# One more landing place for weight words, and copies moved from VectorE to ScalarE in seven items of a fused attention and MLP kernel

## The chip, the cores and the metric

The kernel runs on one core of a Trainium2 chip. The core has TensorE (PE, matrix products into PSUM), VectorE (DVE), ScalarE (ACT), GpSimd (POOL) and SyncE (SP); POOL and SP also issue the DMA transfers here. The metric is the device time of one execution in microseconds, smaller is better; the time given is the median of several runs. One execution of the kernel was recorded by the profiler.

## The reference

Inputs are q, k and v in float32 (8 batches, 8 heads, 576 rows, 64 columns) and two weight matrices in float64. Linear attention is followed by a two-layer network with a self-made gate:

```python
q_s = softmax(q, axis=-1)                       # over the 64 columns
k_s = softmax(k, axis=2)                        # over the 576 rows
kv = einsum('bhsd,bhse->bhde', k_s, v)
x = einsum('bhsd,bhde->bhse', q_s, kv)          # then to 4608 tokens x 512
h = x @ w_in                                    # 512 x 2048
sp = maximum(h, 0) + log1p(exp(-abs(h)))        # softplus
out = (h * erf(sp)) @ w_out                     # 2048 x 512
```

## The kernel before

**Items.** The 4608 tokens are cut into 12 blocks of 384, and the 2048 inner columns into 4 groups of 512. A pair of block and group is an item, 48 in all, numbered n. Item n does its first products (`mm1`: x times a group of w_in into banks X, Y and Z of PSUM, evacuated into a tile H), then softplus and erf by ScalarE (`T`, `G`; tile G), then G times H by VectorE (`U`, L1077), and then its second products (`mm2`: G times a group of w_out into banks o). The loop at the end emits, for each n, the first products of item n, the gate of item n-1 and the second products of item n-2; steps of the attention for later blocks are put between (`pace`).

**Two arithmetics.** Items 0 to 4 (n < N32) run in float32. From item 5 on a value is split into a float16 upper half and a float16 remainder, and a product is three float16 products. There `mm1` uses seven smaller products in place of eight: twelve matmuls of 192 columns each, into Y, X, Z, X, X, Z, X. Bank X has one buffer and is written by five of the seven products. Copies and additions between them, by VectorE and ScalarE, build H: the copy of bank Y into H is L1009 on VectorE. G's upper half is a conversion to float16 (`ghi`, L1091, VectorE), its remainder a subtraction (`glo`, L1095, VectorE).

**Weights.** A weight arrives as a 64-bit float: two 32-bit words. Each of 8 weight groups (JOBS) comes in two loads of 1 MB; `wdecode` turns the words of one load into float32 by three integer operations of VectorE (L213, L216, L219), the steps `D0.0` to `D7.1` of the hand-written ORDER. The words land in places that are free at that time: the list `slots` holds them, `rw` and parts of weight tiles WT that are not in use yet, and `wload` gives the next place to the next load. The first eight loads are issued by SP, the others by POOL, each when a decoding has freed its place. After all decodings the weights' scales are found (`Z`) and the weights are split in halves (`S`, `R`; L299 by ScalarE and L300 by VectorE), most of it between items 4 and 9 (SPLITS).

**Order.** ORDER and the loop give the order in which the program is written. A scheduler then orders the instructions of each engine by priorities and by its own estimates; on the chip each engine runs its list in order and waits by semaphores only for what its instruction reads or overwrites. `tc.issue_after(...)` is a hint to the scheduler.

**Start.** SP loads k, q, v and the first words. VectorE makes maxima over k (L517, L518, L521), PE transposes them (kT), VectorE reduces (km) and PE spreads them over the rows (kB). Behind kB stand 46 matmuls without a use of their result, which warm the clock (L809).

Of the kernel before, what the change touches and what calls it, by code (L numbers as in the profile page):

```python
# [10 lines left out]
I32 = mybir.dt.int32  # L11
BF16 = mybir.dt.bfloat16
AF = mybir.ActivationFunctionType
ALU = mybir.AluOpType
# [28 lines left out]

N32 = 5
SPLITS = {4: "", 5: "S1 R1 S2", 6: "S3 R3 S4", 7: "S6 f2 f3", 8: "S5 R5", 9: "S7"}

SHARES = [2.51, 0, 0.16, 0.09, 1.58, 2.43, 1.12, 0.26, 0.29, 0.04, 0.78, 1.12, 0.16]
LEAD = 2.0
# [7 lines left out]
def attn_moe_kernel(  # L56
# [9 lines left out]
    nc = tc.nc  # L66
# [3 lines left out]
    P = 128  # L70
# [43 lines left out]
    WT = [  # L114
        cp.tile([P, 2 * (7 if which == "in" else 4) * 512], F16, name=f"wt{i}")
        for i, (which, g) in enumerate(JOBS)
    ]
# [33 lines left out]
    raws, stg = {}, {}  # L151
    wready = set()
    slots, nxt = [], [0]
# [5 lines left out]
    def wload():  # L159


        i = nxt[0]
        while i < NPC * NJ and slots:
            w = slots.pop(0)
            if i >= NPC * (NJ - 1 if w is None else NJ if w < 2 else w - 2):
                continue
            if w == -1:
                w, other = None, "x7"
            else:
                other = None  # L170
            which, g = wjobs[i // NPC]
            a = i % NPC
            if which == "in":
                src = w_in[a * 2 * P:(a + 1) * 2 * P, 2 * g * 512:2 * (g + 1) * 512]
            else:
                src = w_out[(4 * g + 2 * a) * P:(4 * g + 2 * a + 2) * P, :]
            if other:

                raws[i] = xp.tile([P, 2, 1024], I32, tag=other, name=f"raw_{i}")
            elif w is None:  # L180
                raws[i] = rw.bitcast(I32).rearrange("p (a n) -> p a n", a=2)
            else:
                raws[i] = WT[w][:, :4096].bitcast(I32).rearrange("p (a n) -> p a n", a=2)
            held[i] = -1 if other else w

            eng = nc.sync if i < LOADS.count("w") else nc.gpsimd
            eng.dma_start(raws[i], src.rearrange("(a p) n -> p a n", p=P))
            nxt[0] += 1
            return

    decoded = [None]

    def wdecode(i, part=None):


        jn, a = divmod(i, NPC)
        if jn not in stg:
            if jn + 2 < NJ:
                stg[jn] = WT[jn + 2][:, :4096].bitcast(F32)
            elif jn == NJ - 2:  # L200
                stg[jn] = xp.tile([P, 2048], F32, tag="x7", name=f"sg_{jn}")
            else:
                stg[jn] = rw
        d = stg[jn][:, a * 1024:(a + 1) * 1024].bitcast(I32)
        if part is None:
            r = raws[i].rearrange("p a n -> p (a n)").rearrange("p (n two) -> p n two", two=2)
        else:
            r = raws[i][:, :, 512 * part:512 * part + 512].rearrange(
                "p a (n two) -> p a n two", two=2
            )  # L210
            d = d.rearrange("p (a n) -> p a n", a=2)[:, :, 256 * part:256 * part + 256]
        lo, hi = r[..., 0], r[..., 1]
        nc.vector.tensor_scalar(  # L213
            d, hi, 5, 2, op0=ALU.logical_shift_left, op1=ALU.logical_shift_right,
        )
        nc.vector.scalar_tensor_tensor(  # L216
            d, lo, 29, d, op0=ALU.logical_shift_right, op1=ALU.bitwise_or
        )
        decoded[0] = nc.vector.scalar_tensor_tensor(  # L219
            d, hi, -(2**30), d, op0=ALU.bitwise_and, op1=ALU.bitwise_or  # L220
        )
        if part == 0:
            return
        raws.pop(i)
        h = held.pop(i)
        if h != -1:
            slots.append(h)
        wload()

    def whalf(jn, h):  # L230

        return WT[jn][:, h * 2048:(h + 1) * 2048]

    def wop(jn, h, i, n):

        o = h * WIN + i * 512
        return WT[jn][:, o:o + n * 512].rearrange("p (n c f) -> p n c f", n=n, c=2)
# [735 lines left out]
    def mm1(n, k):  # L973

        p, bk, g = seq[n]
        s = st[n]
        assert ("in", g) in wready
        x = x7[p * NBK + bk]  # L980
        jn = wjobs.index(("in", g))
        Th = T // 2
        if k == 0:
            s["H"] = ch.tile([P, FG, T], F32, tag="H", bufs=3, name=f"H_{n}")
        C = {(i, j): s["H"][:, 2 * i:2 * i + 2, Th * j:Th * j + Th]
             for i in range(2) for j in range(2)}

        def prod(b, wi, xi):
            new = b not in s
            if new:  # L990
                s[b] = psh.tile([P, 512], F32, tag=f"p{b}", name=f"p{b}_{n}")
            w = [wop(jn, h, wi, 1)[:, 0] for h in range(2)]
            for a in range(2):
                o = s[b][:, a * Th:(a + 1) * Th]
                for c in range(2):
                    for i, (wl, xl) in enumerate(((0, 0), (0, 1), (1, 0))):
                        nc.tensor.matmul(  # L997
                            o, w[wl][:, c, a * P:(a + 1) * P], x[:, xl, xi, c, :],
                            start=(new and a == 0 and c == 0 and i == 0),
                            stop=(c == 1 and i == 2), skip_group_check=True,  # L1000
                        )

        def bank2(b):
            return s[b][:, :T].rearrange("p (a t) -> p a t", a=2)

        add = nc.vector.tensor_tensor
        if k == 0:
            prod("Y", 1, 1)
            nc.vector.tensor_copy(C[0, 0], bank2("Y"))  # L1009
            prod("X", 0, 0)  # L1010
            add(C[0, 0], bank2("X"), C[0, 0], op=ALU.add)  # L1011
        elif k == 1:
            prod("Z", 6, 3)
            nc.scalar.copy(C[1, 1], bank2("Z"))
            prod("X", 3, 6)
            nc.scalar.copy(C[0, 1], bank2("X"))
        elif k == 2:
            prod("X", 5, 5)
            add(C[1, 1], bank2("X"), C[1, 1], op=ALU.add)  # L1019
        else:  # L1020
            prod("Z", 4, 2)
            add(C[0, 1], bank2("Z"), C[0, 1], op=ALU.add)  # L1022
            prod("X", 2, 4)
            nc.scalar.copy(C[1, 0], bank2("X"))  # L1024
# [27 lines left out]
    def flat(t):  # L1052
        return t.rearrange("p f t -> p (f t)")
# [34 lines left out]

    def ghi(n):
        s = st[n]  # L1090
        nc.vector.tensor_copy(flat(s["gh"]), flat(s["G"]))  # L1091

    def glo(n):
        s = st[n]
# [48 lines left out]

    steps = start()
    fn = dict(T=softplus, G=erf, U=gmul, I=ghi, O=glo)
    emitted_steps = set()
    done = set()
# [76 lines left out]
    for n in range(N32, N + 2):  # L1224
# [3 lines left out]
        for i in range(4):  # L1228
# [7 lines left out]
            if m2 and i < 3:  # L1236
                tok(f"M{n - 2}.{i}")
                pace(n + (i + 1) / NTT)
        for o in SPLITS.get(n, "").split():
            tok(o)  # L1240
# [35 lines left out]
```

## Time and profile before

| | |
|---|---|
| time, median of 3 runs | 832.39 us (832.22 to 834.11) |
| the profiled execution | 833.08 us, span 831.2 us |
| TensorE busy | 804.8 us (97%) |
| VectorE busy | 626.6 us (75%) |
| ScalarE busy | 503.4 us (61%) |
| moved by DMA | 61.56 MB, 74 GB/s in the mean |

Rows of the timeline give start and length in us, the engine, the line of the program, the operation, output and input, and a count; a bracket holds the engine's idle time before the row and what ended it. Rows of groups give the busy us of all, the mean ns of one, and the idle time before them. Rows of windows give for each engine its busy us in the stretch, then the clock that TensorE was granted (1.00 is full), the mean busy share of the DMA engines and the GB/s that they moved. Rows of DMA issues give the queue, the count, the KB of one and the median us from issue to landing.

### The profile page before, as it was taken

What the parts mean: (1) busy time and instruction counts of PE and PEld (TensorE: products, weight loads), DVE (VectorE), ACT (ScalarE), POOL (GpSimd) and SP (SyncE); (2) the same over time, 40 slices, a digit from 0 to 9 for tenths busy, and PEclk for the clock granted to TensorE, in tenths of its full rate; (3) what the DMA queues carried; (4) which work ended last, traced back from release to release, by engine and by line L of the source; (5) the groups of instructions that cost most, each with busy time, mean ns of one, the idle gap of its engine ahead of it and who ended that gap; (6) DMA issues with size and microseconds to landing.
All of it is one profiled execution on the core that took longest, in us unless ns stands there. A gap on an engine that the chain in (4) does not pass through costs nothing.

```text
span 831.2 us, 15665 instructions
## 1 busy us (share of the span) xinstructions
PE 804.8 (97%) x6610; PEld 546.8 (66%) x6610; DVE 626.6 (75%) x894; ACT 503.4 (61%) x644; POOL 15.9 (2%) x37
## 2 busy tenths in 40 slices
PE   5999999999999999999999999999999999999996
PEld 4555556666676667667767667767776777767762
DVE  6999899999997869757976779867875656544643
ACT  3697678886576656546744746645764555544442
POOL 2101000000000000000000000000000000000000
PEclk9999999999999999999999999999999999999999
DMA  9995721041146206111451205311220100100101
GB/s 248 409 227 181 194 51 39 2 108 40 51 71 140 77 6 137 56 26 27 100 123 39 64 1 109 89 27 27 65 51 15 39 1 2 39 1 2 39 1 39
DMA packets 141349, 61.56 MB, mean 74 GB/s; under 512 B 130528, under 2 KB 132576, under 8 KB 141280
## 3 DMA queue, kind: packets, MB, share of 16 engines
q1 hardware_dynamic: 139104, 52.18, 25.0%
q0 software_dynamic: 2176, 8.39, 2.8%
q8 instruction: 52, 0.85, 0.4%
q14 instruction: 17, 0.14, 0.1%
HBM read 45.09 MB, written 9.44 MB: 66 GB/s over the span
## 4 chain that ended last, share of the span: by engine, by line
PE 55%; DVE 27%; ACT 9%; issue 3%; DMA 3%; SPq 3%; POOL 0%; ACTq 0%; DVEq 0%; POOLq 0%
PE o L1123 27%; PE pX L997 13%; PE pZ L997 7%; DVE G L1077 3%; PE pY L997 3%; ACT G L348 3%; ACT L348 3%; DVE H L1095 3%; DVE wt L300 2%; SPq L419 2%; DVE x L300 2%; DMA q<-in_q_dram 2%; DVE H L1091 2%; DVE x L392 1%; PE x L679 1%
## 5 line engine op out<-in xcount | busy, mean ns | idle before, releaser
L1123 PE MATMUL o<-wt,H 128*128 128x512 f16 x1548 | 356.0, 379 | 1.7 <-DVE H L1091 1.3
L997 PEld LDWEIGHTS <-wt 128*128 128x128 f16 x3612 | 300.0, 98 | 36.5 <-issue 14.3
L1123 PEld LDWEIGHTS <-H 128*128 128x128 f16 x1548 | 149.2, 98 | 154.0 <-DVE H L1091 1.8
L997 PE MATMUL pX<-x,wt 128*128 128x192 f16 x2064 | 198.8, 246 | 3.8 <-DVE H L1019 2.4
L348 ACT ACT_TABLE_LOAD x104 | 133.4, 1283 | 7.0 <-DVE H L1022 5.2
L1077 DVE SCALAR_TENSOR_TENSOR G<-G,small,H 128x1536 f32<-128x1536 f32 x44 | 79.9, 1817 | 53.3 <-ACT G L348 53.0
L1024 ACT COPY H<-pX 128x384 f32<-128x384 f32 x43 | 20.4, 475 | 144.5 <-PE pX L997 141.4
L997 PE MATMUL pZ<-x,wt 128*128 128x192 f16 x1032 | 100.6, 246 | 0.0
L348 ACT ACTIVATE G<-H,U 128x768 f32<-128x768 f32 (+1 forms) x58 | 71.0, 1241 | 22.1 <-DVE H L1022 21.5
L1095 DVE TENSOR_TENSOR H<-G,H 128x1536 f16<-128x1536 f32 x43 | 75.5, 1755 | 0.8
L348 ACT ACTIVATE G<-G 128x1536 f32<-128x1536 f32 x48 | 71.3, 1485 | 0.5
L997 PE MATMUL pY<-x,wt 128*128 128x192 f16 x516 | 49.6, 246 | 0.3 <-DVE H L1009 0.3
L453 ACT ACTIVATE x<-x 128x384 f32<-128x384 f32 (+1 forms) x52 | 16.2, 397 | 48.4 <-PE x L679 48.4
L1022 DVE TENSOR_TENSOR H<-pZ,H 128x384 f32<-128x384 f32 x43 | 23.7, 551 | 26.2 <-PE pZ L997 26.2
L1009 DVE COPY H<-pY 128x384 f32<-128x384 f32 x43 | 23.8, 553 | 25.7 <-PE pY L997 25.7
L299 ACT ACTIVATE x<-x 128x768 f16<-128x768 f32 (+1 forms) x44 | 32.9, 765 | 15.2 <-DVE x L392 15.1
L1091 DVE CAST H<-G 128x1536 f16<-128x1536 f32 x43 | 41.1, 957 | 0.8
L300 DVE SCALAR_TENSOR_TENSOR x<-x,x 128x768 f16<-128x768 f32 (+1 forms) x44 | 37.3, 852 | 3.2 <-ACT x L299 3.2
L1139 DVE TENSOR_SCALAR ob<-o,V 128x512 f32<-128x512 f32 x29 | 21.7, 748 | 20.4 <-PE o L1123 20.4
L1011 DVE TENSOR_TENSOR H<-pX,H 128x384 f32<-128x384 f32 x43 | 23.9, 555 | 13.2 <-PE pX L997 12.4
L464 DVE TENSOR_REDUCE q_m<-q 128x16 f32<-128x1024 f32 x14 | 17.0, 1217 | 17.0 <-DMA q<-in_q_dram 16.8
L1036 PE MATMUL pX<-x,wt 128*128 128x384 f32 x80 | 28.3, 488 | 0.2 <-DVE wt L219 0.2
(183 smaller groups left out, 790.4 us busy)
## 6 DMA issues: line engine op xcount, KB each, us to landing
out_dram<-ob SPq DMA_DIRECT2D x32, 256.0 KB, 2.3
vbuf<-in_v_dram SPq DMA_DIRECT2D x56, 128.0 KB, 3.2
q<-in_q_dram SPq DMA_DIRECT2D x56, 128.0 KB, 3.2
k<-in_k_dram SPq DMA_DIRECT2D x56, 128.0 KB, 3.2
wt<-in_moe_w_out_dram POOLq DMA_DIRECT2D x5, 1024.0 KB, 6.6
wt<-in_moe_w_in_dram SPq DMA_DIRECT2D x4, 1024.0 KB, 11.9
wt<-in_moe_w_out_dram SPq DMA_DIRECT2D x2, 1024.0 KB, 15.5
H_raw<-in_k_dram SPq DMA_DIRECT2D x2, 512.0 KB, 4.8
```

Source lines behind the costliest of these rows:

```text
L299: nc.scalar.activation(hi, src, AF.Copy, scale=s)
L300: nc.vector.scalar_tensor_tensor(lo, src, s, hi, op0=ALU.mult, op1=ALU.subtract)
L348: i = nc.scalar.activation(out_, in_, func, **kw)
L997: nc.tensor.matmul(o, w[wl][:, c, a * P:(a + 1) * P], x[:, xl, xi, c, :], start=(new and a == 0 and c == 0 and i == 0), stop=(c == 1 and i ...
L1009: nc.vector.tensor_copy(C[0, 0], bank2("Y"))
L1011: add(C[0, 0], bank2("X"), C[0, 0], op=ALU.add)
L1022: add(C[0, 1], bank2("Z"), C[0, 1], op=ALU.add)
L1036: nc.tensor.matmul(ph[:, :T], w[:, c, a * P:(a + 1) * P], x[:, c, :], start=(c == 0), stop=(c == NC4 - 1),)
L1077: nc.vector.scalar_tensor_tensor(flat(s["G"]), flat(s["G"]), GA32 if n < N32 else GA[:, g:g + 1], flat(s["H"]), op0=ALU.mult, op1=ALU.mult,)
L1091: nc.vector.tensor_copy(flat(s["gh"]), flat(s["G"]))
L1095: nc.vector.tensor_tensor(flat(s["gl"]), flat(s["G"]), flat(s["gh"]), op=ALU.subtract)
L1123: nc.tensor.matmul(o, s[gt][:, a, ts_], w[wl][:, a, :], start=(first_ and a == 0 and i == 0), stop=(last_ and a == FG - 1 and i == 2),)
```

## The change

First, behind the decoding of load 6 (the seventh, `D3.0`) one more place is put into `slots`: the upper thousand words of two weight tiles, WT[1] and WT[3] (columns 4096 to 6144), which together hold the 1 MB of one load. Load 11 goes there in two transfers; it is decoded in two halves of 512 words a row (six operations in place of three). The loads after it each take the place that the load before them had. Second, in items 5 to 11 (RELIEF) the copy of bank Y and the conversion to G's upper half are done by ScalarE in place of VectorE.

```diff
+RELIEF = range(5, 12)
...
             if w == -1:
                 w, other = None, "x7"
-            else:
-                other = None
+            elif w == -2:
+                w, other = None, "upper"
...
+            if other == "upper":
+                raws[i] = [WT[o][:, 4096:6144].bitcast(I32) for o in (1, 3)]
+            elif other:
...
             eng = nc.sync if i < LOADS.count("w") else nc.gpsimd
-            eng.dma_start(raws[i], src.rearrange("(a p) n -> p a n", p=P))
+            src = src.rearrange("(a p) n -> p a n", p=P)
+            if other == "upper":
+                for h in range(2):
+                    eng.dma_start(raws[i][h], src[:, h])
+            else:
+                eng.dma_start(raws[i], src)
...
+        if type(raws[i]) is list:
+            pieces = [(r, d[:, 512 * h:512 * h + 512]) for h, r in enumerate(raws[i])]
...
+        for r, d in pieces:
...
         wload()
+        if i == 6:
+            slots.append(-2)
+            with tc.issue_after(decoded[0].ins):
+                wload()
...
-            nc.vector.tensor_copy(C[0, 0], bank2("Y"))
+            (nc.scalar.copy if n in RELIEF else nc.vector.tensor_copy)(C[0, 0], bank2("Y"))
...
-        nc.vector.tensor_copy(flat(s["gh"]), flat(s["G"]))
+        (nc.scalar.copy if n in RELIEF else nc.vector.tensor_copy)(flat(s["gh"]), flat(s["G"]))
```

The scheduler makes more of it than the diff shows. The first place is POOL's list at the start of the program; wt_90 and wt_92 are WT[1] and WT[3], and the last two rows are the first loads that POOL issues after the start. Before:

```order
L444 MEMSET vtail 64x8
L411 MEMSET wt_89 128x16
L406 MEMSET v_1_114 128x16
L857 TENSOR_TENSOR q_0_134<-H_raw_q,q_0_m 128x4x128 x2
L857 TENSOR_TENSOR q_1_135<-G_raw_1_108,q_1_m 128x4x128 x2
L443 MEMSET vtail 64x520
L444 MEMSET vtail 64x8
L187 DMA rw<-in_moe_w_out_dram 128x2x1024
```

After:

```order
L467 MEMSET vtail 64x8
L434 MEMSET wt_89 128x16
L197 DMA wt_90<-in_moe_w_in_dram 128x1024
L429 MEMSET v_1_114 128x16
L197 DMA wt_92<-in_moe_w_in_dram 128x1024
L880 TENSOR_TENSOR q_0_134<-H_raw_q,q_0_m 128x4x128 x2
L880 TENSOR_TENSOR q_1_135<-G_raw_1_108,q_1_m 128x4x128 x2
L466 MEMSET vtail 64x520
```

The two transfers of load 11 stand ahead of everything that POOL computes, and no wait stands in front of them.

The second place is ScalarE's list from the softplus of item 7 on. H_1217 and G_1459 (after: H_1221, G_1463) are item 7's tiles, H_1466 (H_1470) and G_1650 (G_1654) are item 8's, H_1658 is item 9's. Before:

```order
L348 ACTIVATE G_1459<-G_1459 128x1536
L1014 COPY H_1466<-pZ_1523 128x2x192
L299 ACTIVATE wt_94<-wt_96,small 128x1024
L1016 COPY H_1466<-pX_1481 128x2x192
L299 ACTIVATE wt_94<-wt_96,small 128x1024
L654 CAST asc<-qT_0_1568 128x512
L654 CAST asc<-qT_1_1600 128x512
L1024 COPY H_1466<-pX_1481 128x2x192
L348 ACT_TABLE_LOAD
L348 ACTIVATE G_1650<-H_1466,U_673 128x1536
L299 ACTIVATE wt_96<-rw,small 128x2048
```

After:

```order
L371 ACTIVATE G_1463<-G_1463 128x1536
L1037 COPY H_1470<-pZ_1527 128x2x192
L1039 COPY H_1470<-pX_1485 128x2x192
L322 ACTIVATE wt_96<-rw,small 128x2048
L1114 CAST H_1221<-G_1463 128x1536
L677 CAST asc<-qT_1_1604 128x512
L677 CAST asc<-qT_0_1572 128x512
L1047 COPY H_1470<-pX_1485 128x2x192
L1032 COPY H_1658<-pY_1659 128x2x192
L371 ACT_TABLE_LOAD
L371 ACTIVATE G_1654<-H_1470,U_678 128x1536
```

The long split of 2048 columns moved from behind item 8's softplus to a place ahead of the conversion of item 7's G; that conversion, new here, stands between the two copies of item 8's bank X, and the copy of item 9's bank Y ahead of item 8's softplus.

More of the change, by code (lines that the diff above doesn't have):

```diff
@@ L166, in wload @@
                 continue
+            other = None
             if w == -1:
                 w, other = None, "x7"
-            else:
-                other = None
+            elif w == -2:
+                w, other = None, "upper"
             which, g = wjobs[i // NPC]
@@ L176, in wload @@
                 src = w_out[(4 * g + 2 * a) * P:(4 * g + 2 * a + 2) * P, :]
-            if other:
+            if other == "upper":
+                raws[i] = [WT[o][:, 4096:6144].bitcast(I32) for o in (1, 3)]
+            elif other:
                 raws[i] = xp.tile([P, 2, 1024], I32, tag=other, name=f"raw_{i}")
@@ L204, in wdecode @@
         d = stg[jn][:, a * 1024:(a + 1) * 1024].bitcast(I32)
-        if part is None:
-            r = raws[i].rearrange("p a n -> p (a n)").rearrange("p (n two) -> p n two", two=2)
-        else:
-            r = raws[i][:, :, 512 * part:512 * part + 512].rearrange(
-                "p a (n two) -> p a n two", two=2
-            )
[L211 to L221, printed above, removed]
+        if type(raws[i]) is list:
+            pieces = [(r, d[:, 512 * h:512 * h + 512]) for h, r in enumerate(raws[i])]
+        elif part is None:
+            pieces = [(raws[i].rearrange("p a n -> p (a n)"), d)]
+        else:
+            pieces = [(
+                raws[i][:, :, 512 * part:512 * part + 512],
+                d.rearrange("p (a n) -> p a n", a=2)[:, :, 256 * part:256 * part + 256],
+            )]
+        for r, d in pieces:
+            if part is None:
+                r = r.rearrange("p (n two) -> p n two", two=2)
+            else:
+                r = r.rearrange("p a (n two) -> p a n two", two=2)
+            lo, hi = r[..., 0], r[..., 1]
+            nc.vector.tensor_scalar(
+                d, hi, 5, 2, op0=ALU.logical_shift_left, op1=ALU.logical_shift_right,
+            )
+            nc.vector.scalar_tensor_tensor(
+                d, lo, 29, d, op0=ALU.logical_shift_right, op1=ALU.bitwise_or
+            )
+            decoded[0] = nc.vector.scalar_tensor_tensor(
+                d, hi, -(2**30), d, op0=ALU.bitwise_and, op1=ALU.bitwise_or
+            )
         if part == 0:
```

## The prediction

> **What bounds the kernel now.** I read the engine shares first, then the busy times over the items that the change touches, then TensorE's timeline for its gaps, and last the first 26 us, because the built order puts a part of the change there.
>
> ```profile
> PE 804.8 (97%) x6610; PEld 546.8 (66%) x6610; DVE 626.6 (75%) x894; ACT 503.4 (61%) x644; POOL 15.9 (2%) x37
> ```
>
> TensorE (PE) is busy for 97% of the span: a change is worth only what it takes from PE's idle time or adds to it. Next the busy times from the first product of item 5 to that of item 12, cut in the timeline where an item's first product (pY) starts; items 5 and 6 are woven together, so the first window holds both.
>
> ```profile
> core 0: us, PE busy (x) PEld busy (x) DVE busy (x) ACT busy (x) POOL busy (x), PEclk, DMA share, GB/s
> 132.40:158.75 26.35, 25.52 (x198) 18.48 (x197) 26.29 (x32) 21.18 (x23) 0.00 (x0) 1.00 0.03 13
> 158.75:178.24 19.49, 18.66 (x206) 13.51 (x205) 19.42 (x31) 15.96 (x18) 0.63 (x2) 1.00 0.27 61
> 178.24:193.93 15.69, 15.69 (x133) 11.53 (x131) 15.69 (x30) 10.29 (x12) 0.00 (x0) 1.00 0.33 75
> 193.93:212.89 18.96, 17.55 (x155) 11.69 (x154) 17.96 (x23) 12.81 (x20) 0.00 (x0) 1.00 0.34 91
> 212.89:229.81 16.92, 15.78 (x130) 11.33 (x129) 16.58 (x22) 10.53 (x13) 0.00 (x0) 1.00 0.01 5
> 229.81:247.36 17.55, 17.55 (x203) 12.77 (x201) 15.93 (x27) 13.52 (x15) 0.63 (x2) 1.00 0.31 70
> ```
>
> VectorE (DVE) has next to no slack until 230 us, ScalarE (ACT) is busy for three quarters, and PE's clock is granted in full. What PE loses to that stands in its timeline; a bracket holds the idle time before the row and what ended it.
>
> ```profile
> 136.00 1.15 PE L997 MATMUL pY<-x,wt 128*128 128x192 f16 x12 [0.27 <-DVE H L1009]
> 137.67 1.16 PE L997 MATMUL pX<-x,wt 128*128 128x192 f16 x12 [0.51 <-DVE H L1011]
> ...
> 169.12 0.75 PE L564 MATMUL kv<-vbuf,k 128*64 128x65 f32 x16 [0.64 <-ACT k L348]
> ...
> 203.14 0.66 PE L661 MATMUL qT<-ident,q 128*128 128x128 f32 x4 [1.41 <-ACT x L453]
> ...
> 227.51 0.65 PE L543 MATMUL kB<-ident,km 128*128 128x128 f32 x4 [1.14 <-DVE km L532]
> ```
>
> These sum to 0.27 + 0.51 + 0.64 + 1.41 + 1.14 = 3.97 us. Modelled ends hide a little more (12 products are drawn 1.15 us long, though the next group follows after 0.99 where nothing waits): 5 x 0.16 more, so **4.8 us** is all that a perfect relief of DVE can win in these items.
>
> **The change, part by part.** *The load.* In the source it stands behind the seventh decoding. In the built order its two halves stand on POOL's queue between two small memsets at the program's start, and wait for nothing. The memset in question is the first row below; the others are the loads that POOL issues before the change, and one of SP's.
>
> ```profile
> 2.00 0.12 POOL L406 MEMSET v<- 128x16 f32 x1
> ...
> 30.03 0.89 POOL L187 DMA_DIRECT2D rw<-in_moe_w_out_dram  x1 [6.96 <-DVE x_e L127]
> ...
> 64.95 0.71 POOL L187 DMA_DIRECT2D rw<-in_moe_w_in_dram  x1 [29.50 <-DVE wt L219]
> ```
>
> ```profile
> 20.28 2.29 SPq L187 DMA_DIRECT2D raw<-in_moe_w_in_dram  x1
> ```
>
> ```profile
> rw<-in_moe_w_out_dram POOLq DMA_DIRECT2D x1, 1024.0 KB, 9.9
> ...
> raw<-in_moe_w_in_dram SPq DMA_DIRECT2D x1, 1024.0 KB, 23.7
> ...
> rw<-in_moe_w_in_dram POOLq DMA_DIRECT2D x1, 1024.0 KB, 5.4
> ```
>
> So what came at 64.95 now comes at about 2 us, and there k and q are on their way:
>
> ```profile
> 4.88 0.69 DVE L517 TENSOR_TENSOR asc<-H_raw 128x512 f32<-128x512 f32 x1 [4.88 <-DMA H_raw<-in_k_dram]
> ...
> 6.78 0.69 DVE L517 TENSOR_TENSOR asc<-H_raw 128x512 f32<-128x512 f32 x1 [0.76 <-DMA H_raw<-in_k_dram]
> ...
> 8.28 0.68 DVE L521 TENSOR_TENSOR asc<-asc,kt 64x512 f32<-64x512 f32 x1 [0.35 <-DMA kt<-in_k_dram]
> ```
>
> ```profile
> 4.00:6.00 2.00, 0.00 (x0) 0.00 (x0) 1.09 (x2) 0.00 (x0) 0.00 (x0) 1.00 1.13 348
> 6.00:8.00 2.00, 0.00 (x0) 0.00 (x0) 1.14 (x3) 0.00 (x0) 0.00 (x0) 1.00 1.19 200
> ...
> 30.00:35.00 5.00, 5.00 (x17) 2.96 (x16) 5.00 (x11) 4.78 (x15) 1.87 (x3) 1.00 1.03 409
> ```
>
> DVE's first maxima wait three times for k, and the DMA engines are full meanwhile (shares over 1). A load of POOL's doesn't queue behind SP's: the one issued at 30.03 landed 9.9 us later, near 40, the one that SP had issued at 20.28 after 23.7, at 44. So the new 1 MB takes its part from k. Its price is at most its own time: 1.05 MB at the 409 GB/s of 30 to 35 us is 2.6 us, at the mean of 348 and 200 it is 3.8; at least it is nothing, if k's rows pass first. Alone, such a load took 5.4 us, 2.8 more than its transfer; I put 1.8 of that ahead of the data, which then flow from 3.8 us. At half the rate from there k's second half lands some 1.5 us later, its tail (the wait at 8.28) about 2.1, and q, behind it, up to 2.6. I take **2.2 us**, near the full transfer, since the landings show sharing.
>
> Does PE lose all of it? The maxima are followed by a chain without a hole: 46 matmuls that warm the clock stand behind kB, made from the maxima, and the first item waits for a DVE that is full from 16 us on.
>
> ```profile
> 11.89 6.71 PE L809 MATMUL warm<-ident 128*128 128x256 f16 x46
> ...
> 25.86 1.53 PE L1036 MATMUL pX<-x,wt 128*128 128x384 f32 x4 [0.24 <-DVE wt L219]
> ```
>
> So 25.86 becomes 28.1. SP's later words shift with it and stay off the path.
>
> One rule speaks against this change: the Trainium skill (DMA: Bandwidth & Descriptors, Queues, rings and completion order) has every DMA engine alternate between queues by whole packets, about 9 to 17 descriptors long. By it and the page's 436 GB/s (Anatomy of one DMA) POOL's 1 MB would pass ahead of most of k, an estimate of 2.4 us for the loss and 0.2 on top of the sum below. The two landings, 9.9 and 23.7 us, agree with alternation; no row shows its grain.
>
> *What the early words bring.* One wait of DVE's, in the second-last pair of decodings, goes, since each later load moves up one place:
>
> ```profile
> 97.10 0.69 DVE L213 TENSOR_SCALAR rw<-wt 128x1024 int32<-128x1024 int32 x1 [3.83 <-DMA wt<-in_moe_w_out_dram]
> ```
>
> ```profile
> 100.00:120.00 20.00, 19.49 (x80) 10.11 (x79) 18.74 (x42) 15.28 (x34) 0.00 (x0) 1.00 0.23 53
> ```
>
> The last load still waits for the decoding before it, so part of the 3.83 us comes back there. PE has its products of items 3 and 4 queued and idles 0.51 us in the whole window behind it, and the weights' scales wait for matmuls that stand in PE's order at 111 us. I price this at 0, with 0.5 us as the most. The decoding in halves costs DVE three more instructions:
>
> ```profile
> 24.30 0.69 DVE L216 SCALAR_TENSOR_TENSOR wt<-rw,wt 128x512 int32<-128x512 int32 x1
> ...
> 78.99 1.22 DVE L216 SCALAR_TENSOR_TENSOR wt<-rw,wt 128x1024 int32<-128x1024 int32 x1
> ```
>
> Twice 0.69 against 1.22 is 0.16 us for an operation, some 0.5 us for three. PE's second products of items 1 and 2 cover it; without that cover it is 0.5 us more.
>
> *Copies and upper halves in items 5 to 11.*
>
> ```profile
> L1091 DVE CAST H<-G 128x1536 f16<-128x1536 f32 x43 | 41.1, 957 | 0.8
> L1009 DVE COPY H<-pY 128x384 f32<-128x384 f32 x43 | 23.8, 553 | 25.7 <-PE pY L997 25.7
> ```
>
> ```profile
> L348 ACT ACTIVATE G<-G 128x1536 f32<-128x1536 f32 x48 | 71.3, 1485 | 0.5
> L1016 ACT COPY H<-pX 128x384 f32<-128x384 f32 x43 | 20.6, 480 | 3.5 <-DVE G L1077 1.5 <-PE pX L997 1.4
> L629 ACT CAST rw<-q 128x1024 f16<-128x1024 f32 x10 | 10.4, 1047 | 2.1 <-DVE q L478 2.1
> ```
>
> DVE loses 7 x (0.957 + 0.553) = 10.6 us. ACT's price for the cast isn't in the trace: 1.485 us (erf on as many elements) to 1.57 (1.047 x 1.5); I take 1.5. So ACT gains 7 x (1.5 + 0.48) = 13.9 us. Over the 115 us of the six windows DVE goes from 111.9 busy us to 101.3 (88%), ACT from 84.3 to 98.2 (85%). Neither is the bound by its sum, but ACT now waits in order: the cast needs G's product from DVE, and behind the cast stand copies of bank X, which PE needs before its next product there.
>
> To price that I laid the built order of PE, ACT and DVE on the durations of before's rows, each instruction after its engine's previous one and after what it reads. Without the shift at the start, the first product comes at 158.7 for item 7 (before 158.75), 177.4 for item 8 (178.24), 194.1 for item 9 (193.93), 212.3 for item 10 (212.89), 227.9 for item 11 (229.81), 245.6 for item 12 (247.36). Gained are the wait at 227.51, since DVE reaches km with a copy and a cast less in front, and half of the one at 203.14, since a long split of ACT's moves ahead. Lost is about 0.7 us in item 8, where PE waits for an addition of DVE's that now stands behind a split of 2048 elements and G's lower half; the waits at 136 and 137.67 become one of 1.2 us and one of 0.4. The sum is **-1.8 us**; the bounds are -4.8 (all idle gone) and, above, the second rival.
>
> *Sum.* 2.2 + 0 - 1.8 = +0.4 us. The profiled execution took 833.08 us (span 831.2), so its like takes 833.5; the median of the three runs is 832.39, and I forecast **832.8**, which is no change: 0.3% of this time, about what a measurement of this kernel can tell from none, is 2.5 us.
>
> **The rivals.** *First, faster:* the load slips in front of nothing, because k's small rows are served first, and the relief wins most of its 4.8 us. For it: PE's five idles all name DVE or ACT behind DVE. Against it: the 9.9 us landing. With 0 and -3.6 the time is 828.8; it needs more than 2.5 us in all. *Second, slower:* ACT becomes the bound in items 5 to 11. Place: the copies of bank X behind the casts. For it: the kernel's own waits at 169.12 and 203.14 are for ACT already. Against it: second products, 2.6 us a piece, stand between most X products. If PE waits half a cast in each of seven items, that is 7 x 0.75 = 5.2 us in place of the gain, and with the start 832.4 + 2.2 + 5.2 = 839.8. It decides from 0.3 us an item, 2.1 us in all, that the walk has missed. *Third, slower:* the load costs its whole transfer, 2.6 to 3.8 us, and the relief turns into other waits of the same size: 835.0 to 836.2. *That the change doesn't do what it says* is part of the forecast: the load isn't behind the seventh decoding.
>
> **How the numbers follow.** Forecast, both terms nearly cancelling (830 to 834.8): 0.63. First rival 0.14, second 0.12, third 0.11. The range takes the first rival's middle and the third whole, and leaves the second out: 829.0 to 836.2. Faster by over 0.3% is the first rival and a sliver of the forecast, 0.15; slower the second and third, 0.23; within 0.3% the rest, 0.62.
>
> **What would show it.** Right at the start: DVE's tail row of k at about 10.4 in place of 8.28, the warming matmuls at 14, the first item's product at 28.1; if they stand where they stood, the first term is wrong. No wait for words near 97 us, and a short one before the last decoding. From item 5's first product to item 12's 113.2 us in place of 115.0, ACT near 85% there; an idle of PE's in each item that names ACT would show the second rival. From item 12 on nothing should change but the offset.

## The result, and the profile after

| | before | after |
|---|---|---|
| time, median | 833.25 us (832.22 to 834.90) | 840.06 us (838.64 to 841.30) |
| ratio of the times | | 1.0078, 95% interval 1.0059 to 1.0097 |
| the profiled execution | 833.08 us, span 831.2 us | 841.30 us, span 839.5 us |
| VectorE, ScalarE busy | 626.6, 503.4 us | 618.4, 515.2 us |

The change makes the kernel 0.8% slower, and 840.06 us lies outside the predicted range of 829.0 to 836.2. Where the 8.2 us between the two profiled executions arise is read from TensorE's timelines: the start of each item's first product (pY) after, less the same start before, worked out from the two. The profiled execution is the slowest of the change's four, so its parts add up to more than the 6.8 us between the medians.

| at the start of | first product on x | item 5 | 12 and 13 | 14 | 15 | 16 | 30 to 47 |
|---|---|---|---|---|---|---|---|
| later by (us) | 4.86 | 4.75 | 4.69 | 5.58 | 6.98 | 8.23 | 8.2 |

So the program's start costs 4.9 us, items 5 to 12, for which the relief was made, give nothing, and items 13 to 15 cost another 3.5 us. These three places are shown in turn.

**The start.** The timelines of VectorE, GpSimd and TensorE after, in this order:

```profile
6.37 0.69 DVE L540 TENSOR_TENSOR asc<-H_raw 128x512 f32<-128x512 f32 x1 [0.40 <-DMA H_raw<-in_k_dram]
...
13.02 0.68 DVE L544 TENSOR_TENSOR asc<-asc,kt 64x512 f32<-64x512 f32 x1 [5.51 <-DMA kt<-in_k_dram]
```

```profile
2.00 0.68 POOL L197 DMA_DIRECT2D wt<-in_moe_w_in_dram  x1
...
2.73 0.55 POOL L197 DMA_DIRECT2D wt<-in_moe_w_in_dram  x1
```

```profile
16.63 7.60 PE L832 MATMUL warm<-ident 128*128 128x256 f16 x46
...
30.72 1.56 PE L1059 MATMUL pX<-x,wt 128*128 128x384 f32 x4
```

The words' two transfers are issued at 2 us. The two halves of k are as early as before (6.37 us against 6.78), but VectorE waits 5.51 us for k's tail and reads it at 13.02 us in place of 8.28. The DMA issues of the first 16 us, after and then before (KB of one transfer, median us from issue to landing), and the DMA queues from 6.5 to 8.0 us after (packets, MB, share of the engines; q0 is POOL's queue, q1 is SP's):

```profile
H_raw<-in_k_dram SPq DMA_DIRECT2D x2, 512.0 KB, 4.5
wt<-in_moe_w_in_dram POOLq DMA_DIRECT2D x2, 512.0 KB, 8.9
...
kt<-in_k_dram SPq DMA_DIRECT2D x2, 128.0 KB, 11.1
```

```profile
kt<-in_k_dram SPq DMA_DIRECT2D x2, 128.0 KB, 6.4
```

```profile
q0 software_dynamic: 102, 0.38, 84.0%
q1 hardware_dynamic: 263, 0.07, 20.3%
```

The tail lands 11.1 us after its issue in place of 6.4. In the window in which it is due, POOL's queue moves 0.38 MB in 102 packets and SP's 0.07 MB in 263: packets of the tail hold one row of 256 bytes, those of the words nearly 4 KB in the mean. SP's queue keeps the larger number of packets and gets a sixth of the bytes.

**Items 5 to 12.** The windows of the six stretches from item 5's first product to item 12's are summed in the first row; then TensorE's largest idles there.

```profile
sum 114.90, PE 111.24 PEld 79.68 DVE 104.27 ACT 94.41 POOL 1.26; mean PE 18.54 PEld 13.28 DVE 17.38 ACT 15.74 POOL 0.21
```

```profile
141.54 1.15 PE L1020 MATMUL pX<-x,wt 128*128 128x192 f16 x12 [0.76 <-DVE H L1034]
...
144.34 1.15 PE L1020 MATMUL pX<-x,wt 128*128 128x192 f16 x12 [0.16 <-ACT H L1039]
...
173.60 0.76 PE L587 MATMUL kv<-vbuf,k 128*64 128x65 f32 x16 [0.70 <-ACT k L371]
...
181.65 0.62 PE L587 MATMUL kv<-vbuf,k 128*64 128x65 f32 x13 [0.31 <-DMA vbuf<-in_v_dram]
...
199.84 1.15 PE L1020 MATMUL pX<-x,wt 128*128 128x192 f16 x12 [0.74 <-DVE H L1042]
...
208.17 0.65 PE L684 MATMUL qT<-ident,q 128*128 128x128 f32 x4 [0.94 <-ACT x L476]
```

The stretch takes 114.90 us against 114.96 before (247.36 less 132.40). VectorE is busy for 91% of it and ScalarE for 82%. The waits of 1.14 us (km) and 0.27 us are gone and that of 1.41 us is 0.94, but 0.74 us at an addition of VectorE's and 0.31 us for v are new. PE's idle time falls from 4.21 to 3.66 us (114.90 - 111.24, and the same from the windows before), and its busy time, in which the ends are modelled, rises by 0.49. What this rise hides isn't shown; the stretch is as long as it was.

**Items 13 to 15.** The chain from item 11's conversion to the q tail, on ScalarE, VectorE and SP's queue in order of time, after and then before:

```profile
260.53 1.47 ACT L1114 CAST H<-G 128x1536 f16<-128x1536 f32 x1 [1.14 <-DVE G L1100]
...
261.91 0.70 ACT L652 CAST asc<-qt 128x256 f16<-128x256 f32 x2
...
262.03 1.76 DVE L1118 TENSOR_TENSOR H<-G,H 128x1536 f16<-128x1536 f32 x1 [0.83 <-ACT H L1114]
263.71 0.75 DVE L653 TENSOR_TENSOR asc<-qt,asc 128x256 f16<-128x256 f32 x2
...
264.49 1.23 SPq L655 DMA_TRANSPOSE qt<-asc  x1
...
267.65 0.42 DVE L541 TENSOR_TENSOR asc<-asc 128x256 f32<-128x256 f32 x1 [2.72 <-DMA qt<-asc]
```

```profile
255.94 2.95 SPq L632 DMA_TRANSPOSE q<-rw  x1
...
256.01 0.71 ACT L629 CAST asc<-qt 128x256 f16<-128x256 f32 x2 [1.30 <-DVE kvh L607]
...
256.76 0.75 DVE L630 TENSOR_TENSOR asc<-qt,asc 128x256 f16<-128x256 f32 x2
...
258.99 1.26 SPq L632 DMA_TRANSPOSE qt<-asc  x1
...
262.08 0.43 DVE L518 TENSOR_TENSOR asc<-asc 128x256 f32<-128x256 f32 x1 [2.13 <-DMA qt<-asc]
```

The conversion (L1114) waits 1.14 us for G's product, and the subtraction that makes G's remainder on VectorE (L1118) waits 0.83 us for the conversion. Behind the remainder stands the subtraction for the q tail (L653), which before (L630) came ahead of it. It ends at 264.46, and 0.03 us later the transposing transfer of the tail starts, 0.8 us late beyond the offset of 4.69. Before, this transfer started when SP's transpose ahead of it had ended, at 258.90. The two casts of the q tail stand behind the conversion on ScalarE and are 5.90 us later than before, but they end at 262.61, so the transfer doesn't wait for them. VectorE's row behind the transposes is 0.9 us late beyond the offset, and with it the additions to bank X that stand behind it in VectorE's order. Then TensorE after, its one row of before that answers to the 2.19 us, VectorE's wait for the next q after and before, and the windows after around the start of item 15 (the column behind POOL's is the granted clock):

```profile
278.41 1.15 PE L1020 MATMUL pX<-x,wt 128*128 128x192 f16 x12 [0.76 <-ACT H L1039]
...
300.92 1.60 PE L1020 MATMUL pX<-x,wt 128*128 128x192 f16 x12 [2.19 <-DVE H L1042]
302.31 2.13 PE L1020 MATMUL pY<-x,wt 128*128 128x192 f16 x12
```

```profile
294.34 1.15 PE L997 MATMUL pX<-x,wt 128*128 128x192 f16 x12 [1.20 <-DVE H L1019]
```

```profile
291.78 1.22 DVE L487 TENSOR_REDUCE q_m<-q 128x16 f32<-128x1024 f32 x1 [3.04 <-DMA q<-in_q_dram]
```

```profile
285.21 1.22 DVE L464 TENSOR_REDUCE q_m<-q 128x16 f32<-128x1024 f32 x1 [2.04 <-DMA q<-in_q_dram]
```

```profile
300.00:302.00 2.00, 1.08 (x11) 1.06 (x11) 1.33 (x3) 0.00 (x0) 0.00 (x0) 0.86 0.00 0
302.00:304.00 2.00, 2.00 (x15) 1.89 (x13) 0.00 (x0) 1.43 (x2) 0.00 (x0) 0.50 0.00 0
304.00:306.00 2.00, 2.00 (x18) 1.71 (x17) 0.82 (x2) 1.97 (x3) 0.00 (x0) 0.78 0.00 0
```

An idle of 0.76 us in item 13 brings the offset to 5.58 at item 14. One of 2.19 us before item 14's last group, where the kernel before has 1.20, brings it to 6.98 at item 15: the addition that ends it (L1042) stands in VectorE's list behind the work on the next q, for which VectorE waits 3.04 us in place of 2.04. Then the granted clock falls to 0.50 for 3.41 us (from 301.46 to 304.87), item 15's first twelve products last 2.13 us in place of 1.15, and the offset becomes 8.23. Before, the clock was 1.00 there.

### The profile page after: what moved, and what is told of

The parts are those of the page before. It is cut to its first block, busy times and chain, and to the rows that moved or that the text cites. A ratio compares the mean times of both kernels' runs of the same rounds, so it can differ in the third digit from the quotient of the medians.

```text
span 839.5 us, 15665 instructions
## 1 busy us (share of the span) xinstructions
PE 808.2 (96%) x6610; PEld 549.2 (65%) x6610; DVE 618.4 (74%) x883; ACT 515.2 (61%) x658; POOL 16.3 (2%) x38
## 4 chain that ended last, share of the span: by engine, by line
PE 58%; DVE 20%; ACT 13%; DMA 4%; issue 2%; SPq 2%; ACTq 0%; DVEq 0%
PE o L1146 26%; PE pX L1020 14%; PE pZ L1020 7%; ACT G L371 4%; ACT L371 4%; PE pY L1020 3%; DVE G L1100 3%; DVE H L1118 2%; SPq L442 2%; DMA q<-in_q_dram 2%; DVE x L323 2%; PE kv L587 1%; PE x L702 1%; DMA kt<-in_k_dram 1%; DVE wt L323 1%
## 5 line engine op out<-in xcount | busy, mean ns | idle before, releaser
L1118 DVE TENSOR_TENSOR H<-G,H 128x1536 f16<-128x1536 f32 x43 | 75.5, 1755 | 2.7 <-ACT H L1114 1.9
L1032 DVE COPY H<-pY 128x384 f32<-128x384 f32 x36 | 19.9, 553 | 26.8 <-PE pY L1020 26.8
L1114 DVE CAST H<-G 128x1536 f16<-128x1536 f32 x36 | 34.4, 957 | 0.7
```

The lines of the kernel that those rows point to most:

```text
L1114: (nc.scalar.copy if n in RELIEF else nc.vector.tensor_copy)(flat(s["gh"]), flat(s["G"]))
L1118: nc.vector.tensor_tensor(flat(s["gl"]), flat(s["G"]), flat(s["gh"]), op=ALU.subtract)
```

## The experiments

Times are medians, each beside the kernel before measured with it (833.18 us for the load alone, the load held back, the relief alone and items 5 to 10 without the load; 832.28 for item 11 only and the three kernels with memsets; 832.39 for the other four); intervals are 95%.

### The load alone

```diff
-RELIEF = range(5, 12)
+RELIEF = range(0)
```

> Load 11 in its new place as in the change, copies and casts left on VectorE. Theory: the load costs 4.7 us at the start (the tail rows of k land at 12.9 us in place of 8.2) and nothing later is tied to it, so 832.4 + 4.7 = 837.1, with PE's first product of item 5 near 137.1 and the offset constant from there to the end. Rival: the further 3.5 us that the change loses in items 13 to 16 come from the shifted loads and not from the copies; then 840.5.

Measured: 836.85 us, ratio 1.0047 (1.0031 to 1.0062), 3.7 us more than before. The first key product is 3.71 us late, the first product on x 3.70, item 13 is 3.8 late and the end 4.2. So the start's whole delay reaches the end, with nothing given back by the early words. VectorE's wait for the tail:

```profile
11.99 0.68 DVE L544 TENSOR_TENSOR asc<-asc,kt 64x512 f32<-64x512 f32 x1 [4.39 <-DMA kt<-in_k_dram]
```

The delay is not one number: the tail landed 10.1 us after its issue here, 11.1 in the change's profile, and 10.5 and 10.2 in two more kernels with the same early load (the change without item 11 and the change with twenty memsets, below).

### Half of the load

As the load alone, but the second 512 KB are held by a write into their place behind the seventh decoding.

```diff
+            for o in (3,):
+                with tc.issue_after(decoded[0].ins):
+                    nc.vector.memset(WT[o][:, 4096:4098], 0.0)
             slots.append(-2)
```

> The early load alone (no relief), of which only the first 512 KB go at the program's start and the other 512 KB are held behind the seventh decoding. Theory (the delay grows with the bytes that stand beside k's): first key product 1.6 to 2.2 us late instead of 3.7, time 834.9 to 835.5. Rival A (a cost by having a second queue busy at all while k's tail is fetched): 3 us late or more, 836 to 837. Rival B (the first 512 KB drain before k's tail comes up, the second 512 KB do the harm): under 0.7 us late, 833.3 to 834.3.

Measured: 834.42 us, ratio 1.0020 (1.0011 to 1.0030), 2.0 us over before.

```profile
9.80 0.68 DVE L547 TENSOR_TENSOR asc<-asc,kt 64x512 f32<-64x512 f32 x1 [2.14 <-DMA kt<-in_k_dram]
```

The first key product is 1.52 us late, a little under the theory's 1.6 to 2.2 and less than half of the 3.7 to 4.7 of the whole megabyte. In this profile 0.80 us of it are left at item 5. Both rivals fall: neither a busy second queue alone nor only the second half does the harm. (The expected times were reckoned from 833.2 us for the kernel before, which took 832.39 here.)

### The tail ahead of k

The load alone, with k's tail issued first.

```diff
             if o == "k":
+                d["kt"] = load_tail(k, "kt", 0)
                 for hf in range(2):
                     kx.append(load_raw(k, ch, "H", 3, 0, hf))
-                d["kt"] = load_tail(k, "kt", 0)
```

> The early load alone (no relief), and SyncE issues k's tail before k's two halves instead of behind them; the written order behind it changes a little (the list of ready work is drawn anew). Theory (the tail's two transfers of 256-byte rows, last of k's in the queue, are what the early words delay): the tail lands near 5 to 7 us instead of 11, the halves of k by 7 to 9, the first key product at 9 to 10.5 us, and the time is 833.2 to 834.7. Rival (the early megabyte takes its share of the transfers in whatever order k's come: all of k lands late): first key product at 12 to 13 us, time 836 to 837.

Measured: 840.17 us, ratio 1.0082 (1.0063 to 1.0101). The theory fell, and the rival's size too. The tail landed 3.4 us after its issue, but now k's halves were late:

```profile
9.21 0.69 DVE L540 TENSOR_TENSOR asc<-H_raw 128x512 f32<-128x512 f32 x1 [9.21 <-DMA H_raw<-in_k_dram]
...
12.12 0.69 DVE L540 TENSOR_TENSOR asc<-H_raw 128x512 f32<-128x512 f32 x1 [1.76 <-DMA H_raw<-in_k_dram]
```

The second half is read at 12.12 us in place of 6.78, and the first key product is 5.03 us late. What is delayed is whatever of k comes up once POOL's words flow, not the tail for its small rows alone. Not all of the time is the start's: of the delay 3.35 us were left at item 8, and 4.0 us came at two idles of 2.10 us in items 9 and 10, where the kernel before has 1.41 and 1.14, the second with a dip of the clock behind it; moving the tail also changed the written order there.

### The load held back

The load alone, with both transfers held as above, so that they are issued near 50 us.

```diff
+            for o in (1, 3):
+                with tc.issue_after(decoded[0].ins):
+                    nc.vector.memset(WT[o][:, 4096:4098], 0.0)
             slots.append(-2)
```

> The new landing place with copies and casts left on VectorE; VectorE writes two columns of the place behind the seventh decoding, so that the load can't start before it (two small instructions more). Theory: the start stands where it stood (tail rows of k at 8.2 us, first product at 25.9), the wait of 3.8 us of VectorE near 97 us goes and PE doesn't feel it: 832.4, at best 831.9. Rival: the early words do speed up what follows, then 830 or less.

Measured: 834.46 us, ratio 1.0016 (1.0005 to 1.0027). The start is that of the kernel before (first key product 0.30 us earlier), so the start's loss does come from the early issue. But the theory's 832.4 is missed: 1.3 us by the medians remain, and the profiled execution, 0.5 us late at the end, shows where such a loss can come from: the load now meets k of the next pair of batches.

```profile
50.24 1.09 POOL L197 DMA_DIRECT2D wt<-in_moe_w_in_dram  x2 [15.06 <-DVE wt L251]
```

```profile
49.36 8.98 SPq L445 DMA_DIRECT2D k<-in_k_dram  x8
```

```profile
59.08 0.69 DVE L543 TENSOR_TENSOR asc<-k 128x512 f32<-128x512 f32 x1 [1.08 <-DMA k<-in_k_dram]
```

The same issues in the kernel before:

```profile
50.63 5.34 SPq L419 DMA_DIRECT2D k<-in_k_dram  x8
```

SP's queue stands over them for 8.98 us in place of 5.34, and VectorE waits 1.08 us for k, where it didn't wait. That this makes up all of the 1.3 us isn't shown.

### The relief alone

```diff
-        if i == 6:
-            slots.append(-2)
-            with tc.issue_after(decoded[0].ins):
-                wload()
```

> The copies and casts of items 5 to 11 on ScalarE, without the new landing place. Theory: items 5 to 12 take as long as before, and some 3.5 us are lost in items 13 to 16, since the cast of item 11 on ScalarE stands ahead of the conversion of the q tail, whose transposing transfer then starts later: 832.4 + 3.5 = 835.9. Rival A: without the load the relief shows its own gain, 832.4 - 1.8 = 830.6. Rival B: the late loss belongs to the load, then 832.4.

Measured: 833.93 us, ratio 1.0011 (1.0000 to 1.0023): 0.75 us more than before, between the expectations. Item 12 starts 0.18 us late, so the relief wins nothing in its own items without the load too; item 14 starts 1.08 us late, so 0.90 us are lost behind item 11's conversion.

### Items 5 to 10 only, without the load

As the relief alone, and

```diff
-RELIEF = range(5, 12)
+RELIEF = range(5, 11)
```

> Copies and casts on ScalarE in items 5 to 10 only, without the new landing place. Theory: the loss of some 3.5 us in items 13 to 16 hangs on the cast of item 11 alone, so it goes, and what is left is the relief by itself, 832.4 - 1.8 = 830.6 to 832.4. Rival: the loss comes from all seven items together (a changed order of the whole stretch); then it stays and the time is 835 to 836.

Measured: 832.71 us, ratio 0.9993 (0.9983 to 1.0004). Item 12 is 0.08 us early, item 14 0.11 early: without item 11 the late loss is gone, and what is left can't be told from no change.

### Item 11 only, without the load

```diff
-RELIEF = range(5, 12)
+RELIEF = range(11, 12)
```

> Only item 11's copy and cast go to ScalarE, no early load. Theory (that cast stands ahead of the q tail's two casts on ScalarE and so makes the second tail batch late): item 12 within 0.3 of the kernel before, item 14 late by 0.8 to 1.1 us, and the time 0.8 to 1.3 over the kernel before, 833.9 to 834.5. Rival (the loss at item 14 needs the relief of the items before it): within 0.4 of the kernel before.

Measured: 833.21 us, ratio 1.0014 (1.0004 to 1.0024), 0.9 us more. From item 12 to item 14 the profile loses 0.66 us (0.30 early to 0.36 late), a little less than expected. The loss is item 11's own; it doesn't need the items before it. Both of item 11's operations were moved here, and the trace tells which one costs: in all seven kernels in which ScalarE does item 11's conversion, VectorE's remainder waits 0.83 to 0.84 us for it, and the q tail's transposing transfer starts 0.03 us after the subtraction behind the remainder. In the other seven it starts 0.09 us after SP's transpose ahead of it.

### The change with the load held back

The load (3.7 us) and the relief (0.75 us) together make 4.4 us, and the change lost 6.8. The remainder is asked for here: the whole change, with both transfers held as above.

> The whole change (relief in items 5 to 11), but the words' early load held behind the seventh decoding, so that the program's start is that of the kernel before. It tells whether the 2.4 us by which the change exceeds its parts (6.9 against 3.7 for the load and 0.75 for the relief, on the medians) comes with the early start or with the relief. Theory A (the excess hangs on the early transfers: their shift of the start puts the second half of q's load later against the work of items 14 and 15): first key product at 8.8 to 9.1 us, about +0.7 at item 14, no dip of the granted clock near 300 us, in all 833.9 to 835.3 (the held load alone took 1.3 over the kernel before, the relief alone 0.75). Rival B (the excess comes from the added decoding and the relief together, whatever the start): the dip is there too and the time is 836.5 to 838.

Measured: 836.25 us, ratio 1.0043 (1.0027 to 1.0060), 3.9 us over before. Theory A fell: the start is right (first key product 0.16 us late, item 13 1.11), and yet the long idle and the dip are there.

```profile
297.24 1.20 PE L1023 MATMUL pX<-x,wt 128*128 128x192 f16 x12 [2.10 <-DVE H L1045]
```

```profile
298.00:302.00 4.00, 4.00 (x30) 3.69 (x28) 0.56 (x1) 3.47 (x4) 0.00 (x0) 0.57 0.00 0
```

So the remainder comes with the added decoding and the relief, whatever the start.

### The change without item 11

The change as it is, but RELIEF = range(5, 11).

> The change as it is, with the early load, but item 11's two operations stay on VectorE (relief in items 5 to 10). Theory (item 11's cast on ScalarE is what makes the late loss, by the queue of the q tail's casts behind it): first key product 3.7 to 4.7 late, items 12 to 14 no later than that, no idle over 1.5 us and no dip of the clock near 300 us, and 836.0 to 837.2 in all, the load alone's time less 0.5 at most. Rival (the excess comes from any relief beside the shifted start): 838.5 to 840.

Measured: 837.08 us, ratio 1.0062 (1.0045 to 1.0080), 4.7 us over before, near the theory (its start is 4.13 us late in this profile). No dip, but the idle before item 15 is longer than the 1.5 us that the theory allowed:

```profile
298.37 1.15 PE L1020 MATMUL pX<-x,wt 128*128 128x192 f16 x12 [1.77 <-DVE H L1042]
```

This wait hangs on the second half of the next q, which SP issues ahead of item 15. From SP's first issue of it to VectorE's first row on it passed 6.2 to 6.4 us in the change, in the change held back and here, and 5.2 to 5.7 us in the kernels with the load or the relief alone and in the kernel before. In these three kernels, and in none of the others run up to here, the DMA queues show a packet of kind "instruction" within that stretch. The change, from 289 to 291 us:

```profile
q14 instruction: 1, 0.01, 1.0%
```

I read it as a block of some engine's program being fetched. In the kernel before one comes at 268.5 us, with the relief alone at 287.2, just behind the wait. The relief shortens VectorE's list by 14 instructions, the decoding in halves lengthens it by three; so I took it for VectorE's, moved by these numbers into the wait for q.

### Three and twenty instructions more on VectorE

Memsets of a tile that nobody reads, at the head of VectorE's list, where it waits for k until 4.9 us. On all engines the order is else that of the kernel they are put into, but for two neighbouring products of kv on TensorE, near 178 us, which the traces with twenty memsets show in the other order.

```diff
+    nop = cp.tile([P, 4], F32, name="nop")
+    for _ in range(20):
+        nc.vector.memset(nop, 0.0)
```

Twenty in the change (idle before item 15 stands for the one before item 14's last group):

> The change as it is, and twenty memsets of 128x4 more on VectorE before its first work, while it waits for k; nothing else moves on any engine. They push the place at which VectorE's instruction stream is fetched in blocks. Theory (in the changed kernel the fetch, one packet of the instruction queue at 289.7 us, falls into the wait for the second half of q and delays that transfer's end, so that TensorE's idle before item 15 passes 2 us and the clock is cut to 0.50 for 3 us): the packet comes 10 to 25 us earlier, the last of q's four transfers lands after 3.4 to 3.9 us instead of 4.2, the idle before item 15 is 1.1 to 1.7 us, the granted clock stays at 1.0 from 296 to 310 us, and the time is 837.2 to 838.4. Rival (the fetch has no part; load and relief together make q late in another way): idle and dip as in the change, 839.3 to 841.

Measured: 837.40 us, ratio 1.0053 (1.0041 to 1.0065), as the theory expected. Over the kernel before that is 5.1 us, against 6.8 for the change. All five executions (836.10 to 837.97) are faster than the change's four (838.64 to 841.30). The packet moved to 271.5 us, the slowest of q's four transfers landed 3.5 us after its issue in place of 4.2, the idle fell from 2.19 to 1.08 us, and the clock stayed at 1.00. The rows are the landings of q's four transfers in the change and with twenty memsets (least, median, most), and the idle.

```profile
DMA to landing us min/median/max: 3.2/3.5/4.2
```

```profile
DMA to landing us min/median/max: 3.1/3.4/3.5
```

```profile
298.41 1.15 PE L1023 MATMUL pX<-x,wt 128*128 128x192 f16 x12 [1.08 <-DVE H L1045]
```

Three in the relief alone, as many as the decoding in halves adds:

> The relief alone (items 5 to 11, no early load), and three memsets of 128x4 more on VectorE before its first work; they stand for the three instructions by which the split decoding lengthens VectorE's stream in the change, and cost VectorE nothing there, since it waits for k. Theory (the place of the fetch decides): the packet of the instruction queue moves from 287.0 us into the wait for q, 282 to 286 us; the last of q's four transfers lands after 4.0 to 4.3 us instead of 3.4, the idle before item 15 grows from 1.07 to 1.8 to 2.2 us, and the time is 834.6 without and 836.0 to 836.6 with a dip of the granted clock behind it. Rival: three memsets change nothing, 833.5 to 834.3, as for the relief alone.

Measured: 834.81 us, ratio 1.0026 (1.0012 to 1.0039). Three memsets that VectorE has time for move the packet to 286.4 us, into the wait for q. The slowest transfer lands after 4.0 us, not 3.4, and the idle goes from 1.07 to 2.08 us, with a dip behind it; item 16 starts 4.5 us later than before in place of 0.95, though part of that (1.1 us by item 13) arose before the wait.

```profile
297.20 1.31 PE L1019 MATMUL pX<-x,wt 128*128 128x192 f16 x12 [2.08 <-DVE H L1041]
```

```profile
298.00:300.00 2.00, 2.00 (x16) 1.90 (x14) 0.00 (x0) 1.44 (x2) 0.00 (x0) 0.51 0.00 0
```

The median moves less than the profiled execution (836.49 us) and stays short of the theory's 836.0: executions with a mean granted clock of 0.998 or less took 834.96 us and more, those above it 834.67 and less, about half of each. So the dip seems to come in some executions and not in others, though only one was traced.

Twenty in the relief alone:

> The control to the three memsets: the relief alone with twenty memsets of 128x4 on VectorE before its first work. Theory (the place of the fetch decides, not the memsets): the packet comes at 262 to 278 us, away from the wait for q, the idle before item 15 stays at 1.0 to 1.4 us, no dip there, and the time is 833.3 to 834.4. Rival (added instructions cost by themselves): slower than with three, 836 or more.

Measured: 833.02 us, ratio 1.0010 (0.9995 to 1.0026), as the relief alone. The packet is at 267.0 us, the idle before item 15 0.96 us, and no dip. The added instructions themselves cost nothing; where they put the fetch does. The medians with three and with twenty differ by 1.8 us, though their intervals against the kernel before overlap; the wait for q and the idle in the traces say it more clearly than the times.

## Why the prediction was wrong

*What bounds the kernel.* TensorE did remain the bound (PE is busy 96% of the longer span), and each loss was an idle of PE's or a slower clock, as that reading says.

*The load's price.* Place and mechanism were right: two transfers at POOL's head at 2 us, k delayed, and the chain behind it without a hole (4.74 us at the first key product, 4.86 at the first product on x). The size was wrong: 2.2 us taken and 3.8 as the most, 4.86 in the change's profile, and 3.70, 4.00 and 4.14 in three other kernels with the whole load at the start. The step that failed is "At half the rate from there k's second half lands some 1.5 us later, its tail (the wait at 8.28) about 2.1". Half the rate is not what SP's queue got. k's second half was not late at all, since POOL's queue moved nothing before 5.4 us (3.8 was taken); the tail, alone against them, got 0.07 of 0.45 MB. Alternation by whole packets, which the prediction drew from the Trainium skill (DMA: Bandwidth & Descriptors, Queues, rings and completion order), agrees with the direction; its estimate of 2.4 us was as short as mine.

*The early words.* Right. The wait of 3.83 us is gone, 1.95 us of it come back at a later decoding, and TensorE gains nothing.

```profile
103.70 0.69 DVE L232 TENSOR_SCALAR rw<-wt 128x1024 int32<-128x1024 int32 x1 [1.95 <-DMA wt<-in_moe_w_out_dram]
```

*The decoding in halves.* Its 0.5 us were covered, as said: with the load alone the delay is 3.70 us at the first product on x and 3.75 at item 5. Not foreseen: its three instructions, taken with the relief, move a fetch of VectorE's program into the wait for q. The twenty memsets take 1.40 - (-0.13) = 1.53 us of idle and 1.24 us of clock away again by the offsets (6.98 - 5.58 and 8.23 - 6.98 in the change; 4.06 - 4.19 and 4.07 - 4.06 with them).

*The relief in items 5 to 11.* The size of the conversion was right (1.47 us on ScalarE, 1.5 taken), and the loads nearly (91 and 82%, against 88 and 85). So were the waits one by one: km's gone, 1.41 become 0.94, the new one of 0.7 measured at 0.74; the pair of 0.78 us was put at 1.6 and came out at 0.92. But the sum, -1.8 us, was -0.06. The step that failed is "The sum is **-1.8 us**": the idles that it lists gain 1.14 + 0.70 and lose 0.7 + 0.82, 0.3 us in all, and the starts of the items, taken from a walk of my own, did not agree with them. Where the walk had item 8 0.84 us early, it was 0.39 later than item 5's offset. The other runs agree: from item 5 to item 12 the eight kernels with the relief in items 5 to 10 or 11 take 114.39 to 115.53 us, and the kernel before and the three with a load and no relief 114.96 to 115.21 (the tail ahead of k, with its dip there, left aside). With the listed idles alone and the same start the forecast would have been 834.3 us.

*"From item 12 on nothing should change but the offset."* Wrong, by 3.5 us: 0.89 behind item 11's conversion, for which VectorE's remainder and, behind it, the q tail's subtraction wait, 1.40 at the late q, and 1.25 by the clock. I had counted item 11's conversion among ScalarE's sums and not looked at what waits for it on VectorE, past item 12. In the profiled execution the whole sum is 4.86 - 0.11 - 0.06 + 3.54 = 8.23 us, where the prediction has 2.2 + 0 - 1.8 + 0 = 0.4.

*The rivals.* The third, slower, had the mechanism of the first two places (the load at its full price and a relief worth nothing), and 835.0 to 836.2 us is close to the load alone, 836.85. The second had the time, 839.8 us, but not the reason: ScalarE did not become the bound in items 5 to 11. None had the last 2.6 us.

## What to carry to other kernels

The prefetch without a wait in front of it went to the head of its queue here, and its price was paid by the transfer on the critical path that came up next, which got a sixth of the bytes: look at that transfer first, and not at the mean rate. A step that is moved to another engine is to be followed past the last item it was meant for, to what waits for it on every engine and to what stands behind that. And before a sum taken from a walk is believed, it should agree with the sum of the idles that it names.

## What the runs showed of the hardware

**A fetch of program code can delay a transfer.** Three memsets at the start of VectorE's list, where it waits anyhow, made the slowest of q's four transfers land 4.0 us after its issue in place of 3.4, at 288 us of the program, by moving one packet of some 8 KB (0.15 MB in 18 packets over the span). With that packet inside the stretch from issue to use it lasted 6.2 to 6.4 us in four kernels, without it 5.1 to 5.7 in the others. The Trainium skill (DMA: Bandwidth & Descriptors, Queues, rings and completion order) says that a transfer's completion signal lands only after every earlier write of the same DMA engine, across its queues. That would make q's signal wait for a slow code packet. The trace shows more than that: in the change the code packet had ended at 290.25 us, and q's own packets went on to 291.04, at the end one at a time. The DMA queues from 290.25 to 291.05 us after, and over the last 0.8 us of the same transfers before (283.9 to 284.7):

```profile
q1 hardware_dynamic: 30, 0.01, 8.7%
```

```profile
q1 hardware_dynamic: 380, 0.09, 52.4%
```

The last half microsecond of q's data holds 16 to 19 packets in three of the four kernels with the code packet inside (132 in the change held back), and 57 to 386 in the ten without it. As 8.7% is little more than one engine in 16, it looks as if one engine were behind with its part of q. Which of the 16 engines had the code packet, no run here shows.

**The granted clock fell to 0.50 after four of five idles of 2.08 to 2.19 us.** From the timelines and windows of all kernels run, the longest idles of TensorE within its work and the clock behind them:

| kernel | idle ends at | idle, us | lowest granted clock of the 4 us behind it |
|---|---|---|---|
| the change | 300.92 | 2.19 | 0.50 |
| the change, load held back | 297.24 | 2.10 | 0.50 |
| the tail ahead of k | 233.01 | 2.10 | 0.50 |
| the tail ahead of k | 208.05 | 2.10 | 1.00 |
| relief and three memsets | 297.20 | 2.08 | 0.50 |
| the change, load held back | 67.90 | 2.01 | 1.00 |
| the change without item 11 | 298.37 | 1.77 | 1.00 |

A dip costs 1.25 to 1.65 us (the step of the offset from item 15 to 16), so an idle of 2.2 us can cost more than half as much again. The Trainium skill (TensorE: Matmul & The Clock Gate, What's actually happening) has the clock halve after an idle window of about 3.4 us of a free-running count. The 0.50 agrees, and so does the length of the dips, 3.41 us in each of the four; the idle that suffices was shorter here, and what decides between the two idles of 2.10 us stays open.
